# A 2:4 pruned matmul on one Trainium2 core: single half-tile loads, alternating VectorE steps, a halved weight piece, narrower last output pieces

## The chip, the core and the metric

The kernel runs on one core of one Trainium2 chip. A core has five engines with queues of their own: TensorE (PE; its weight loads are shown apart as PEld), VectorE (DVE), ScalarE (ACT), GpSimd (POOL) and SyncE (SP). SP and ACT also issue DMAs, which share 16 DMA engines. The metric is device microseconds of one launch, the median of several runs. Before the change it is 235.76 us (three runs, 235.59 to 236.01).

## The reference

x is 16 x 512 x 1024, w is 1024 x 1024, b has 1024 elements, all bf16. In every group of four consecutive rows of w, and in each column, the two elements of largest magnitude are kept and the others set to zero. Then x is multiplied with that pruned w, and b is added.

```
wg = w.reshape(G, M, D)                      # G = 256 groups of M = 4 rows
mag = jnp.abs(wg)
order = jnp.argsort(mag, 1)
thr = jnp.take_along_axis(mag, order[:, M - N:M - N + 1, :], 1)     # N = 2
mask = (mag >= thr).astype(w.dtype)
wp = (wg * mask).reshape(D, D)
return jnp.einsum("bsd,df->bsf", x, wp) + b
```

## The kernel before

The 8192 rows of x are 64 token tiles of 128. An output tile is 128 x 1024, made as two halves of 512 columns, one PSUM bank each. The contraction over 1024 is eight matmuls of 128.

**Pruning.** w is loaded so that the four members of a group lie on one partition (`wv`, L50): partition p, half g of the contraction (0 or 1), member m, column f. Five loads A to E bring it (L53). The work on it is cut into pieces `(g, first column, end column)` (L51). For each piece the magnitudes are made (token A, `abs_piece`, L109, on VectorE for pieces 0 and 2, on ScalarE for the others). Then `prep_piece` (token P, L120) issues seven VectorE steps: hi and lo (L127, L128: the larger and the smaller of each pair), two steps t (L131, L132: the smaller of the two hi, the larger of the two lo), thr (L134: the larger of these, which is the second largest magnitude of the four), mask (L136) and wp (L137: w times mask). Steps follow one another piece by piece. In the text, h, l, t, u, r, k, p stand for hi, lo, the two t, thr, mask and wp, with the number of the piece behind.

**The front.** While w is being pruned, the first T = 7 token tiles are computed directly from the pieces. x is loaded in half tiles (128 tokens x 512 columns, 128 KB; `load_x`, L73): x0 to x6 are the halves g = 0 of tiles 0 to 6; the halves g = 1 come later. TensorE transposes a half tile with four 128-wide transposes (token Tgt, `transpose_half`, L148), and ScalarE copies the result out of PSUM (L154). Then four matmuls per piece and tile (token Mit, `mm_piece`, L157) add piece i to the bank of tile t. All halves g = 1 go through bank 7, so each transpose of these waits for the copy before it. When the left output half of a tile is done, ScalarE moves it out (token V, L176), which frees the bank for the right half. Token S adds the bias to it on VectorE, token U copies pruned weights by four DMAs into the layout for the main phase (`unpack`, L142), token B issues a DMA transpose of x (`issue_batch`, L192). Eight matmuls on zeros (token W, L105) stand ahead of all.

The order of all this on every engine is the order of the tokens in the string `FRONT` (L208), since each instruction is kept in program order. An engine runs its own instructions strictly in that order.

**Loads.** L80 to L94 issue them on two queues: w_A in halves on SP and ACT, x0-1 on SP, x2-3 on ACT, w_B on SP, x4-5 on ACT, and then on SP x6, the g = 1 half of tiles 0-1, w_C, the g = 1 halves of tiles 2-3 and 4-6, w_D, w_E and the bias.

**The main phase.** Tiles 7 to 63 use x transposed by DMA and the unpacked weights: L248 for the tiles 7 to 11 and for the last tile, L286 for the others. VectorE adds the bias (L184), ACT's queue stores (L188). The last tile (`last_tile`, L256) is made in four pieces of 256 columns, each with its own eight matmuls, its add on VectorE (L264) and its store on SP's queue (L265).

The two lists that the change rewrites in the front stand so before:

```
pieces = [(0, 0, 128), (0, 128, 256), (0, 256, 512), (1, 0, 256), (1, 256, 512),
          (0, 512, 768), (0, 768, 1024), (1, 512, 1024)]
load_x(0, 0, 2)
load_x(0, 2, 4, nc.scalar)
load_w("B")
load_x(0, 4, 6, nc.scalar)
load_x(0, 6, 7)
```

Of the kernel before, what the change touches and what calls it, by code (L numbers as in the profile page):

```python
# [10 lines left out]
def kernel(  # L11
# [21 lines left out]
    FH = 512  # L33
# [3 lines left out]
    of = out.flatten_outer_dims()  # L37
# [3 lines left out]
    const = ctx.enter_context(tc.tile_pool(name="const", bufs=1))  # L41
    tmp = ctx.enter_context(tc.tile_pool(name="tmp", bufs=2))
# [4 lines left out]
    bank = [psum.tile([P, FH], fp32, name=f"bank{i}") for i in range(8)]  # L47


    wv = w.rearrange("(g p m) f -> p g m f", g=2, m=4)  # L50
    pieces = [(0, 0, 128), (0, 128, 256), (0, 256, 512), (1, 0, 256), (1, 256, 512),  # L51
              (0, 512, 768), (0, 768, 1024), (1, 512, 1024)]
    loads = {"A": (0, 0, 256), "B": (0, 256, 512), "C": (1, 0, 512), "D": (0, 512, 1024), "E": (1, 512, 1024)}  # L53
    w_ld = {k: const.tile([P, 4, c1 - c0], bf16, name=f"w_{k}") for k, (g, c0, c1) in loads.items()}
    wp_gh = {(g, h): const.tile([P, 4, FH], bf16, name=f"wp_{g}_{h}") for g in range(2) for h in range(2)}

    def w_of(i):
        g, c0, c1 = pieces[i]
# [14 lines left out]
    def load_x(g, ta, tb, eng=nc.sync):  # L73
        xt = const.tile([P, tb - ta, KH], bf16, name=f"xh_{g}_{ta}")
        src = xf[ta * P:tb * P, g * KH:(g + 1) * KH].rearrange("(t p) c -> p t c", p=P)
        K(eng.dma_start(xt[:], src))  # L76
        for t in range(ta, tb):
            xh[(g, t)] = xt[:, t - ta, :]

    load_w("A", nc.sync, 0, 2)  # L80
    load_w("A", nc.scalar, 2, 4)
    load_x(0, 0, 2)
    load_x(0, 2, 4, nc.scalar)
    load_w("B")
    load_x(0, 4, 6, nc.scalar)
    load_x(0, 6, 7)
    load_x(1, 0, 2)
    load_w("C")
    load_x(1, 2, 4)
# [3 lines left out]
    bias_sb = const.tile([P, Dout], bf16, name="bias_sb")  # L93
# [10 lines left out]
        for _ in range(n):  # L104
            K(nc.tensor.matmul(bank[7][:], lhsT=zeros[:, :P], rhs=zeros[:], start=True, stop=True))  # L105

    mags = {}

    def abs_piece(i, on_act):  # L109
        g, c0, c1 = pieces[i]  # L110
        n = c1 - c0
        mag = const.tile([P, 4, n], bf16, name=f"mag_{i}")[:]
        if on_act:
            K(nc.scalar.activation(mag, w_of(i), Act.Abs))  # L114
        else:
            K(nc.vector.tensor_single_scalar(  # L116
                mag.bitcast(u16), w_of(i).bitcast(u16), 0x7FFF, op=Alu.bitwise_and))
        mags[i] = mag

    def prep_piece(i):  # L120
        g, c0, c1 = pieces[i]
        n = c1 - c0
        mag = mags.pop(i)
        magv = mag.rearrange("p (a j) f -> p a j f", j=2)
        hi = tmp.tile([P, 2, FH], bf16, name="hi")[:, :, :n]
        lo = tmp.tile([P, 2, FH], bf16, name="lo")[:, :, :n]
        K(nc.vector.tensor_tensor(hi, magv[:, :, 0, :], magv[:, :, 1, :], op=Alu.max))  # L127
        K(nc.vector.tensor_tensor(lo, magv[:, :, 0, :], magv[:, :, 1, :], op=Alu.min))  # L128
        t1 = tmp.tile([P, FH], bf16, name="t1")[:, :n]
        t2 = tmp.tile([P, FH], bf16, name="t2")[:, :n]  # L130
        K(nc.vector.tensor_tensor(t1, hi[:, 0, :], hi[:, 1, :], op=Alu.min))  # L131
        K(nc.vector.tensor_tensor(t2, lo[:, 0, :], lo[:, 1, :], op=Alu.max))  # L132
        thr = tmp.tile([P, FH], bf16, name="thr")[:, :n]
        K(nc.vector.tensor_tensor(thr, t1, t2, op=Alu.max))  # L134
        mask = tmp.tile([P, 4, FH], bf16, name="mask")[:, :, :n]
        K(nc.vector.tensor_tensor(mask, mag, thr[:, None, :].to_broadcast([P, 4, n]), op=Alu.is_ge))  # L136
        K(nc.vector.tensor_tensor(wp_of(i), w_of(i), mask, op=Alu.mult))  # L137
# [19 lines left out]
    def mm_piece(i, t, start=False, stop=False):  # L157
        g, c0, c1 = pieces[i]
        o = c0 % FH
        for m in range(4):  # L160
            K(nc.tensor.matmul(  # L161
                bank[t][:, o:o + c1 - c0], lhsT=xT[(g, t)][:, m, :], rhs=wp_of(i)[:, m, :],
                start=start and m == 0, stop=stop and m == 3))
# [28 lines left out]
    def issue_batch(t0, nb):  # L192
# [13 lines left out]


    FRONT = """  # L208
        W W W W W W W W A0 A1 T00 T01 T02 T03 P0 M00 M01 M02 P1 T04 T05 A2 M03 M10 T06 M11 M04 M12 T10 M05 M06
        M13 M14 A3 T11 M15 M16 P2 M20 M21 A4 T12 M22 M23 M24 A5 T13 P3 M25 M26 M30 A6 T14 M31 M32 M33 A7  # L210
        P4 T15 M34 M40 M41 M42 V0 M43 V1 T16 M35 V2 M44 P5 B0 U00 U10 M45 V3 M50 V4 M36 V5 M51 M46 P6
        U01 M52 V6 M53 M54 M55 M56 M60 M61 M62 M63 M64 P7 U11 B1 B2 M65 M66 S0 S1 S2 S3 S4 S5 S6
    """
    ABS_ON_ACT = (1, 3, 4, 5, 6, 7)
    for tok in FRONT.split():
        k, n = tok[0], [int(c) for c in tok[1:]]
        if k == "W":
            warm(1)
        elif k == "A":
            abs_piece(n[0], n[0] in ABS_ON_ACT)  # L220
        elif k == "P":
            prep_piece(n[0])
        elif k == "T":
            g, t = n
            transpose_half(g, t, t if g == 0 else T)
        elif k == "M":
            i, t = n
            mm_piece(i, t, start=i in (0, 5), stop=i in (4, 7))
        elif k == "V":
            evac_act(n[0])  # L230
        elif k == "S":
            add_staged(n[0], 0)
        elif k == "U":
            unpack(*n)
        elif k == "B":
            issue_batch(*batches[n[0]])

    for t in range(T):
        mm_piece(7, t, stop=True)
        evac_dve(t, 1, t)  # L240
        store(t)

# [3 lines left out]
    def mm_nat(t, h, bk, c0=0, c1=FH):  # L246
        for kt in range(KT):
            K(nc.tensor.matmul(bank[bk][:, :c1 - c0], lhsT=xN[t][:, kt, :], rhs=wp_nat[h][:, kt, c0:c1],  # L248
                               start=kt == 0, stop=kt == KT - 1))

    def next_bank():
        bk = nbk[0] % 8
        nbk[0] += 1
        return bk

    def last_tile(t):  # L256
        o_sb = get_o(t)
        QW = FH // 2
        for h in range(2):
            for c0 in (0, QW):  # L260
                bk = next_bank()
                mm_nat(t, h, bk, c0, c0 + QW)
                f = slice(h * FH + c0, h * FH + c0 + QW)
                K(nc.vector.tensor_tensor(o_sb[:, f], bank[bk][:, :QW], bias_sb[:, f], op=Alu.add))  # L264
                K(nc.sync.dma_start(of[t * P:(t + 1) * P, f], o_sb[:, f]))  # L265
# [55 lines left out]
```

## Time and profile before

| what | us |
|---|---|
| median of three runs | 235.76 (235.59 to 236.01) |
| the profiled execution's own time | 236.1 |
| its span, first to last instruction | 234.3 |
| TensorE busy | 228.1 |
| VectorE busy | 105.7 |
| ScalarE busy | 18.5 |
| w_A landed (SP's half, ACT's half) | 3.64, 3.83 |
| x0-1, x2-3 landed | 5.33, 5.77 |
| x4-5, w_B, x6 landed | 7.57, 8.08, 8.45 |
| w_C, w_D, w_E landed | 10.72, 14.10, 16.48 |
| last store landed | 233.37 |

The span is the time between the first and the last recorded instruction of one profiled execution; what lies around it belongs to the measured time only. A matmul's recorded duration is longer than what it holds TensorE for, since matmuls overlap: in the main phase 512-wide matmuls are recorded with 379 ns each and start 216 ns apart. Starts, not durations, tell the rate. The same holds for VectorE's steps, so the timeline is read by starts.

### The profile page before, as it was taken

The numbers are of one execution on the slowest core, as the hardware profiler recorded it, in microseconds if no ns is written. First come the engines' busy times: TensorE is split into PE (matmuls) and PEld (weight loads), VectorE is DVE, ScalarE is ACT, GpSimd is POOL, SyncE is SP. The second block draws the span as 40 slices with busy tenths as digits, with TensorE's granted clock in tenths as the row PEclk, the third lists the DMA queues.
The fourth block names the chain that finished last, engine by engine and source line by source line (L and its number), as shares of the span: only waits on it lengthen the run. The fifth ranks groups of instructions, "written<-read, shape, count | busy, mean of one in ns | idle before, by whom it ended". The sixth has DMA issues, their size and how long they took to land.

```text
span 234.3 us, 2922 instructions
## 1 busy us (share of the span) xinstructions
PE 228.1 (97%) x1197; PEld 114.6 (49%) x1216; DVE 105.7 (45%) x189; ACT 18.5 (8%) x29; POOL 0.7 (0%) x6
## 2 busy tenths in 40 slices
PE   6999999999999999999999999999999999999994
PEld 2889844444444444444444444444444444444453
DVE  3999995342442343344244234334324424433433
ACT  3899000000000000000000000000000000000000
POOL 1000000000000000000000000000000000000000
DMA  6999799999822399216952289221996221122122
GB/s 174 352 243 236 170 210 187 279 209 349 239 93 92 93 213 276 90 48 160 286 151 77 90 215 278 90 92 55 260 304 195 85 90 73 61 90 92 45 90 90
DMA packets 75292, 38.19 MB, mean 163 GB/s; under 512 B 60176, under 2 KB 67088, under 8 KB 75280
## 3 DMA queue, kind: packets, MB, share of 16 engines
q1 hardware_dynamic: 65392, 20.84, 42.6%
q10 hardware_dynamic: 9888, 17.17, 20.3%
q8 instruction: 9, 0.15, 0.3%
q14 instruction: 3, 0.02, 0.0%
HBM read 4.19 MB, written 16.78 MB: 90 GB/s over the span
## 4 chain that ended last, share of the span: by engine, by line
PE 93%; DMA 3%; DVE 2%; issue 1%; SPq 0%
PE bank L286 75%; PE bank L161 9%; PE bank L248 9%; DMA w_B<-in_w_dram 3%; PE bank L152 1%; DVE mask L136 0%; DVE wp L137 0%; SPq L76 0%; SPq L69 0%; DVE mag L116 0%; DVE o_sb L264 0%; DVE hi L127 0%; DVE lo L128 0%; DVE thr L134 0%; DVE t L132 0%
## 5 line engine op out<-in xcount | busy, mean ns | idle before, releaser
L286 PE MATMUL bank<-wp_nat,xTb 128*128 128x512 bf16 x753 | 165.1, 379 | 0.8
L184 DVE TENSOR_TENSOR o_sb<-bank,bias_sb 128x512 bf16<-128x512 f32 x119 | 76.7, 686 | 119.9 <-PE bank L286 108.6
L286 PEld LDWEIGHTS <-xTb 128*128 128x128 bf16 x768 | 75.1, 98 | 90.6
L161 PE MATMUL bank<-wp,xT 128*128 128x256 bf16 (+2 forms) x223 | 26.6, 272 | 0.4
L161 PEld LDWEIGHTS <-xT 128*128 128x128 bf16 x224 | 19.5, 98 | 5.6 <-ACT xT L154 0.7
L248 PE MATMUL bank<-wp_nat,xTs 128*128 128x512 bf16 (+1 forms) x110 | 21.0, 348 | 0.1
L248 PEld LDWEIGHTS <-xTs 128*128 128x128 bf16 x112 | 11.0, 98 | 10.0
L286 PE MATMUL bank<-wp_nat,xTs 128*128 128x512 bf16 x47 | 10.5, 379 | 0.1
L154 ACT COPY xT<-bank 128x512 bf16<-128x512 bf16 x14 | 7.7, 589 | 1.8 <-PE bank L152 1.8
L286 PEld LDWEIGHTS <-xTs 128*128 128x128 bf16 x48 | 4.7, 97 | 5.7
L136 DVE TENSOR_TENSOR mask<-mag,thr 128x1024 bf16<-128x1024 bf16 (+2 forms) x8 | 5.5, 692 | 0.3
L152 PE MATMUL bank<-ident,xh 128*128 128x128 bf16 x56 | 4.8, 219 | 0.7 <-DMA xh<-in_x_dram 0.6
L152 PEld LDWEIGHTS <-xh 128*128 128x128 bf16 x56 | 3.9, 114 | 1.8 <-DMA xh<-in_x_dram 1.5
L105 PE MATMUL bank<-zeros 128*128 128x512 bf16 x8 | 3.5, 625 | 1.2 <-DVE zeros L97 1.2
L180 DVE TENSOR_TENSOR o_sb<-stage,bias_sb 128x512 bf16<-128x512 f32 x7 | 4.3, 682 | 0.0
L176 ACT COPY stage<-bank 128x512 f32<-128x512 f32 x7 | 3.8, 627 | 0.3 <-PE bank L161 0.3
L127 DVE TENSOR_TENSOR hi<-mag 128x512 bf16<-128x512 bf16 (+2 forms) x8 | 3.4, 420 | 0.4 <-ACT mag L114 0.3
L128 DVE TENSOR_TENSOR lo<-mag 128x512 bf16<-128x512 bf16 (+2 forms) x8 | 3.3, 417 | 0.0
L134 DVE TENSOR_TENSOR thr<-t,t 128x256 bf16<-128x256 bf16 (+2 forms) x8 | 2.3, 292 | 0.3
L105 PEld LDWEIGHTS <-zeros 128*128 128x128 bf16 x8 | 1.0, 140 | 2.8 <-issue 1.7
L131 DVE TENSOR_TENSOR t<-hi 128x256 bf16<-128x256 bf16 (+2 forms) x8 | 2.3, 284 | 0.0
L132 DVE TENSOR_TENSOR t<-lo 128x256 bf16<-128x256 bf16 (+2 forms) x8 | 2.3, 284 | 0.0
(21 smaller groups left out, 17.4 us busy)
## 6 DMA issues: line engine op xcount, KB each, us to landing
out_dram<-o_sb ACTq DMA_DIRECT2D x63, 256.0 KB, 3.4
wp_nat<-wp SPq DMA_DIRECT2D x16, 128.0 KB, 2.7
xh<-in_x_dram SPq DMA_DIRECT2D x3, 256.0 KB, 6.1
xh<-in_x_dram ACTq DMA_DIRECT2D x2, 256.0 KB, 5.2
w_C<-in_w_dram SPq DMA_DIRECT2D x1, 512.0 KB, 6.9
w_D<-in_w_dram SPq DMA_DIRECT2D x1, 512.0 KB, 7.9
w_E<-in_w_dram SPq DMA_DIRECT2D x1, 512.0 KB, 8.9
xh<-in_x_dram SPq DMA_DIRECT2D x1, 384.0 KB, 6.8
```

The source lines that it names most:

```text
L105: K(nc.tensor.matmul(bank[7][:], lhsT=zeros[:, :P], rhs=zeros[:], start=True, stop=True))
L127: K(nc.vector.tensor_tensor(hi, magv[:, :, 0, :], magv[:, :, 1, :], op=Alu.max))
L128: K(nc.vector.tensor_tensor(lo, magv[:, :, 0, :], magv[:, :, 1, :], op=Alu.min))
L136: K(nc.vector.tensor_tensor(mask, mag, thr[:, None, :].to_broadcast([P, 4, n]), op=Alu.is_ge))
L152: K(nc.tensor.transpose(dst[:, m, :], xv[:, m, :], ident[:]))
L154: K(nc.scalar.copy(xt[:], dst))
L161: K(nc.tensor.matmul(bank[t][:, o:o + c1 - c0], lhsT=xT[(g, t)][:, m, :], rhs=wp_of(i)[:, m, :], start=start and m == 0, stop=stop and m = ...
L176: K(nc.scalar.copy(st[:], bank[t][:]))
L180: K(nc.vector.tensor_tensor(get_o(t)[:, h * FH:(h + 1) * FH], stage.pop(t)[:], bias_sb[:, h * FH:(h + 1) * FH], op=Alu.add))
L184: K(nc.vector.tensor_tensor(get_o(t)[:, h * FH:(h + 1) * FH], bank[bk][:], bias_sb[:, h * FH:(h + 1) * FH], op=Alu.add))
L248: K(nc.tensor.matmul(bank[bk][:, :c1 - c0], lhsT=xN[t][:, kt, :], rhs=wp_nat[h][:, kt, c0:c1], start=kt == 0, stop=kt == KT - 1))
L286: K(nc.tensor.matmul(bank[bks[h]][:], lhsT=xN[t][:, kt, :], rhs=wp_nat[h][:, kt, :], start=kt == 0, stop=kt == KT - 1))
```

## The change

Five things are changed.

1. x0 to x4 are each loaded by a DMA of their own, in turn by SP's and ACT's queue; x5 and x6 come together on SP's queue, behind w_B. There are two DMAs more, and ACT's queue carries x1, x3 and x4 instead of x2-3 and x4-5.
2. The third piece, columns 256 to 512 of g = 0, is halved. There are nine pieces, and the numbers of those behind it move up by one: w_C gives pieces 4 and 5, w_D 6 and 7, w_E 8. The magnitudes of pieces 0, 2, 3 and 4 are made on VectorE (token a), the others on ScalarE (token A).
3. A piece's steps are tokens of their own, and the steps of a piece and of its forerunner alternate on VectorE: for example `r4 h5 k4 l5 p4`.
4. The order of the front is written anew with seven W instead of eight; transposes T00 to T04 stand ahead of the first matmul on a piece, and the loop behind the front, which computed the last piece, 7, now computes piece 8.
5. The last tile is made in pieces of 512, 256, 128 and 128 columns.

```
-    pieces = [(0, 0, 128), (0, 128, 256), (0, 256, 512), (1, 0, 256), (1, 256, 512),
+    pieces = [(0, 0, 128), (0, 128, 256), (0, 256, 384), (0, 384, 512), (1, 0, 256), (1, 256, 512),
               (0, 512, 768), (0, 768, 1024), (1, 512, 1024)]
+    H1 = 6
...
-    load_x(0, 0, 2)
-    load_x(0, 2, 4, nc.scalar)
+    load_x(0, 0, 1)
+    load_x(0, 1, 2, nc.scalar)
+    load_x(0, 2, 3)
+    load_x(0, 3, 4, nc.scalar)
     load_w("B")
-    load_x(0, 4, 6, nc.scalar)
-    load_x(0, 6, 7)
+    load_x(0, 4, 5, nc.scalar)
+    load_x(0, 5, 7)
     load_x(1, 0, 2)
     load_w("C")
...
+    def step(k, i):
...
+        if k == "h":
+            K(tt(new(i, "hi", [P, 2, FH])[:, :, :n], mv[:, :, 0, :], mv[:, :, 1, :], op=Alu.max))
+        elif k == "l":
+            K(tt(new(i, "lo", [P, 2, FH])[:, :, :n], mv[:, :, 0, :], mv[:, :, 1, :], op=Alu.min))
...
+        elif k == "k":
+            thr = wk[(i, "thr")][:, :n]
+            K(tt(new(i, "mask", [P, 4, FH])[:, :, :n], mag, thr[:, None, :].to_broadcast([P, 4, n]), op=Alu.is_ge))
+        elif k == "p":
+            K(tt(wp_of(i), w_of(i), wk[(i, "mask")][:, :, :n], op=Alu.mult))
...
     FRONT = """
-        W W W W W W W W A0 A1 T00 T01 T02 T03 P0 M00 M01 M02 P1 T04 T05 A2 M03 M10 T06 M11 M04 M12 T10 M05 M06
-        M13 M14 A3 T11 M15 M16 P2 M20 M21 A4 T12 M22 M23 M24 A5 T13 P3 M25 M26 M30 A6 T14 M31 M32 M33 A7
-        P4 T15 M34 M40 M41 M42 V0 M43 V1 T16 M35 V2 M44 P5 B0 U00 U10 M45 V3 M50 V4 M36 V5 M51 M46 P6
-        U01 M52 V6 M53 M54 M55 M56 M60 M61 M62 M63 M64 P7 U11 B1 B2 M65 M66 S0 S1 S2 S3 S4 S5 S6
+        W W W W W W W a0 A1 h0 l0 T00 t0 u0 T01 r0 k0 T02 p0 T03 T04 h1 M00 l1 t1 M01 u1 M02 r1 k1 M03 a2 p1 T05 T06
+        h2 l2 M04 t2 u2 M10 a3 T10 r2 h3 M05 k2 M11 M06 l3 M12 p2 M13 t3 T11 u3 A5 a4 M14 M15 r3 h4 M16 M20 k3 M21
+        l4 M22 M23 p3 T12 t4 M24 u4 M25 M26 r4 M30 h5 M31 k4 T13 M32 M33 l5 M34 p4 M35 A6 M36 T14 t5 M40 u5 r5 M41
+        h6 A7 M42 k5 T15 l6 M43 A8 p5 M44 t6 M50 u6 r6 M51 h7 M52 k6 M53 V0 l7 T16 V1 B0 U00 U10 p6 M45 M54 t7 u7 V2
+        M55 r7 h8 M46 V3 M60 k7 V4 M56 V5 l8 M61 V6 p7 U01 M62 M63 t8 u8 M64 r8 M65 M66 k8 M70 M71 p8 U11 B1 B2
+        M72 M73 M74 M75 M76 S0 S1 S2 S3 S4 S5 S6
     """
...
     for t in range(T):
-        mm_piece(7, t, stop=True)
+        mm_piece(8, t, stop=True)
...
     def last_tile(t):
         o_sb = get_o(t)
-        QW = FH // 2
-        for h in range(2):
-            for c0 in (0, QW):
+        for h, c0, c1 in ((0, 0, FH), (1, 0, 256), (1, 256, 384), (1, 384, FH)):
...
```

More of the change, by code (lines that the diff above doesn't have):

```diff
@@ L105, in warm, with new @@
             K(nc.tensor.matmul(bank[7][:], lhsT=zeros[:, :P], rhs=zeros[:], start=True, stop=True))
-    mags = {}
-    def abs_piece(i, on_act):
+    wk = {}
+    def new(i, name, shape):
+        wk[(i, name)] = tmp.tile(shape, bf16, name=name)
+        return wk[(i, name)]
+    def step(k, i):
         g, c0, c1 = pieces[i]
         n = c1 - c0
[L112 to L137, printed above, removed]
+        if k in "aA":
+            mag = const.tile([P, 4, n], bf16, name=f"mag_{i}")
+            wk[(i, "mag")] = mag
+            if k == "A":
+                K(nc.scalar.activation(mag[:], w_of(i), Act.Abs))
+            else:
+                K(nc.vector.tensor_single_scalar(
+                    mag[:].bitcast(u16), w_of(i).bitcast(u16), 0x7FFF, op=Alu.bitwise_and))
+            return
@@ new lines, in step @@
+        mag = wk[(i, "mag")][:]
+        mv = mag.rearrange("p (a j) f -> p a j f", j=2)
+        tt = nc.vector.tensor_tensor
+        if k == "h":
+            K(tt(new(i, "hi", [P, 2, FH])[:, :, :n], mv[:, :, 0, :], mv[:, :, 1, :], op=Alu.max))
+        elif k == "l":
+            K(tt(new(i, "lo", [P, 2, FH])[:, :, :n], mv[:, :, 0, :], mv[:, :, 1, :], op=Alu.min))
+        elif k == "t":
+            hi = wk[(i, "hi")]
+            K(tt(new(i, "t1", [P, FH])[:, :n], hi[:, 0, :n], hi[:, 1, :n], op=Alu.min))
+        elif k == "u":
+            lo = wk[(i, "lo")]
+            K(tt(new(i, "t2", [P, FH])[:, :n], lo[:, 0, :n], lo[:, 1, :n], op=Alu.max))
+        elif k == "r":
+            K(tt(new(i, "thr", [P, FH])[:, :n], wk[(i, "t1")][:, :n], wk[(i, "t2")][:, :n], op=Alu.max))
+        elif k == "k":
[3 more added lines that the diff above has]
+            K(tt(wp_of(i), w_of(i), wk[(i, "mask")][:, :, :n], op=Alu.mult))
@@ L208 @@
     FRONT = """
-        W W W W W W W W A0 A1 T00 T01 T02 T03 P0 M00 M01 M02 P1 T04 T05 A2 M03 M10 T06 M11 M04 M12 T10 M05 M06
-        M13 M14 A3 T11 M15 M16 P2 M20 M21 A4 T12 M22 M23 M24 A5 T13 P3 M25 M26 M30 A6 T14 M31 M32 M33 A7
-        P4 T15 M34 M40 M41 M42 V0 M43 V1 T16 M35 V2 M44 P5 B0 U00 U10 M45 V3 M50 V4 M36 V5 M51 M46 P6
-        U01 M52 V6 M53 M54 M55 M56 M60 M61 M62 M63 M64 P7 U11 B1 B2 M65 M66 S0 S1 S2 S3 S4 S5 S6
+        W W W W W W W a0 A1 h0 l0 T00 t0 u0 T01 r0 k0 T02 p0 T03 T04 h1 M00 l1 t1 M01 u1 M02 r1 k1 M03 a2 p1 T05 T06
[4 more added lines that the diff above has]
+        M72 M73 M74 M75 M76 S0 S1 S2 S3 S4 S5 S6
     """
-    ABS_ON_ACT = (1, 3, 4, 5, 6, 7)
     for tok in FRONT.split():
@@ L218 @@
             warm(1)
[L219 to L222, printed above, removed]
+        elif k in "Aahlturkp":
+            step(k, n[0])
         elif k == "T":
@@ L227 @@
             i, t = n
-            mm_piece(i, t, start=i in (0, 5), stop=i in (4, 7))
+            mm_piece(i, t, start=i in (0, H1), stop=i == H1 - 1)
         elif k == "V":
@@ L257, in last_tile @@
         o_sb = get_o(t)
-        QW = FH // 2
-        for h in range(2):
-            for c0 in (0, QW):
[L261 to L265, printed above, removed]
+        for h, c0, c1 in ((0, 0, FH), (1, 0, 256), (1, 256, 384), (1, 384, FH)):
+            bk = next_bank()
+            mm_nat(t, h, bk, c0, c1)
+            f = slice(h * FH + c0, h * FH + c1)
+            K(nc.vector.tensor_tensor(o_sb[:, f], bank[bk][:, :c1 - c0], bias_sb[:, f], op=Alu.add))
+            K(nc.sync.dma_start(of[t * P:(t + 1) * P, f], o_sb[:, f]))
     for bi, (t0, nb) in enumerate(batches):
```

## The prediction

> **What bounds the kernel now.** I read the page's busy times first, then the chain that ended last, in order of time, then the timeline of the first 35 and the last 8 us.
>
> ```profile
> PE 228.1 (97%) x1197; PEld 114.6 (49%) x1216; DVE 105.7 (45%) x189; ACT 18.5 (8%) x29; POOL 0.7 (0%) x6
> ```
>
> TensorE is busy for 97% of the span, and none of its 1024 column blocks is removed. Only its waits can change: before the first transpose, in the front, and after the last matmul. The chain shows where they are:
>
> ```profile
> 1.75 6.33 DMA w_B<-in_w_dram
> ...
> 10.82 0.70 DVE wp L137
> 11.52 0.04 issue
> 11.56 1.03 PE bank L161 x8
> ...
> 34.44 4.96 PE bank L248 x23
> ```
>
> Up to 11.56 us the chain is w_B's landing (1.75 + 6.33 = 8.08) and VectorE's eight steps on piece 2; from there TensorE alone. The timeline gives the steps:
>
> ```profile
> 5.24 0.43 DVE L136 TENSOR_TENSOR mask<-mag,thr 128x512 bf16<-128x512 bf16 x1
> ...
> 5.70 0.43 DVE L137 TENSOR_TENSOR wp<-w_A,mask 128x512 bf16<-128x512 bf16 x1
> ...
> 6.05 0.28 DVE L127 TENSOR_TENSOR hi<-mag 128x256 bf16<-128x256 bf16 x1
> ...
> 10.74 1.06 ACT L114 ACTIVATE mag<-w_C 128x1024 bf16<-128x1024 bf16 x1 [0.27 <-DMA w_C<-in_w_dram]
> ...
> 11.83 0.42 DVE L127 TENSOR_TENSOR hi<-mag 128x512 bf16<-128x512 bf16 x1 [0.32 <-ACT mag L114]
> ```
>
> wp needs the mask and starts 0.03 after it ends (5.24 + 0.43, then 5.70). The next piece's hi needs neither and starts 0.08 before wp ends (5.70 + 0.43 = 6.13, hi at 6.05). So a step with an independent follower holds VectorE for its duration less 83 ns, one with a dependent follower for its duration plus 34: 117 ns apart. With these two rules, the rows' durations and the landings I laid out the front step by step (VectorE's 60 steps, ScalarE's copies, 280 matmuls and transposes): every weight piece comes out within 0.02 us of the trace, every transpose within 0.06, and TensorE's first matmul of L248 at 34.30 (trace: 34.28, record by record; some records are missing, so the chain says 34.44). In that layout VectorE is a second bound: the last piece ends at 28.20 and its first 512-wide matmul starts at 28.24, 0.08 late.
>
> **The change, part by part.**
>
> *Loads.* Two more DMAs, issued at 0.45 to 0.5 us each on queues with room. The eight DMA semaphores go round, so the ninth DMA waits for the first: x5-7 now waits for w_A (landed 3.64 and 3.83), w_C for x1, E for x4. These issues hide behind the transfers in front (the tightest is x5-7: issued by 4.4, and w_B's bytes before it last beyond 6); without that cover each costs its 0.5 us. What counts is the bytes in front. Of the DMA issues (KB, us to landing):
>
> ```profile
> w_B<-in_w_dram SPq DMA_DIRECT2D x1, 256.0 KB, 6.3
> ...
> xh<-in_x_dram SPq DMA_DIRECT2D x1, 128.0 KB, 6.0
> ```
>
> w_B, issued at 1.75, landed at 8.08; x6, issued at 2.47 behind it, at 8.45. x0 should land near 4.2 instead of 5.33 (an estimate: half of its old transfer), x4 near 6.6 (between the old second ACT load at 5.77 and the old third at 7.57). In front of w_B stand 128 KB less, at 350 GB/s (window 6 to 7 us) 0.37 us: 7.72 instead of 8.08. But x5 moves behind w_B: x5-7 ends the same 1408 KB that x6 ended, so it lands at 8.45 as x6 did, and w_C at 10.72. T05 needs x5, so TensorE stands at 8.50 with nine of its 0.224 us units done, where before it had eleven done at 8.57. The earlier x0 buys nothing: 0.73 us of idle time follow x4's work. Bounds for each landing: 0.3 us either way, since two 256 KB loads issued together landed 0.44 apart (5.33, 5.77).
>
> *One warm-up less* saves nothing; TensorE waits for x0 anyway.
>
> *Alternation and the halved piece.* Dependent followers fall from 26 to 13: -1.5 us of VectorE. Halving piece 2 costs 3.44 instead of 2.85 (eight steps at 128 and at 256 columns): +0.59. Piece 4's abs moves from ScalarE to VectorE: +0.34, but VectorE's waits for loads and for ScalarE's abs fall from 0.61 to 0.34. VectorE ends its pieces near 27.34 instead of 28.20, and the 0.08 stall there goes. But the order puts piece 3's steps between piece 4's, and abs 4 waits for w_C. From there to p5 the holds are 0.34 (a4), 1.50 (r3 h4 k3 l4 p3), 0.73 (t4 u4 r4), 1.90 (h5 k4 l5 p4), 0.73, 1.29 (h6 k5 l6) and p5's 0.69: 7.18. With a4 at 10.74, p5 ends at 17.92, M50 starts at 17.97, and what is behind it on TensorE is 23 groups of 256 columns at 0.436, a transpose at 0.224 and 28 matmuls of 512 at 0.2158: 16.30. The front ends at 34.27: **-0.01**. Two more chains are nearly as late. x5-7 at 8.45 brings TensorE to M50 at 17.83, 0.14 spare. w_B at 7.72 frees VectorE for a4 at 10.70, 0.04 spare. The 28 added narrow matmuls cost 28 x (2 x 55.9 - 109) ns = 0.08, inside that sum.
>
> Against the alternation speaks the Trainium skill, VectorE: DVE Perf Modes, "The DRAIN you can't avoid": after every op the pipe must empty before the next, and chaining differently does not help. The hi row above starts 0.08 before its forerunner ends, with nothing left to wait for, so the trace disagrees for independent neighbours (the page itself says further down that an op that isn't held starts earlier). It is a rival below.
>
> *The last tile.*
>
> ```profile
> 229.30 2.85 SPq L265 DMA_DIRECT2D out_dram<-o_sb  x4
> ...
> 231.36 0.42 DVE L264 TENSOR_TENSOR o_sb<-bank,bias_sb 128x256 bf16<-128x256 f32 x1 [0.45 <-PE bank L248]
> ```
>
> The matmul time is the same (8 x 216 + 8 x 109 + 16 x 56 = 3.49; before 32 x 109). The last add shrinks from 0.42 to 0.29 (512 wide 0.69, 256 wide 0.42: 1.05 ns a column). But SP needs 0.34 for an issue and 0.11 to the next (0.046, a semaphore wait of 0.017, 0.046). The 256-wide store is issued 0.43 before the last matmul ends, the third no earlier than 0.02 after, the last no earlier than 0.46 after; now it is 0.48 after. So 0.01 of the 0.13 arrives. The last transfer halves (64 KB took 1.56 to land): -0.05, taken between -0.2 (add and transfer both tell) and +0.1 (256 B rows not shown here).
>
> **Sum:** -0.01 - 0.05 = -0.06. Against the profiled execution (span 234.3, its time 236.1, 1.8 around the span) that is 236.0; the median of the runs is 235.76, 0.3 below that execution, and gets 235.7. As the front's end is the latest of three chains 0.04 to 0.14 apart, one that is late tells and one that is early does not; for landings spread by 0.3 I add 0.1: **235.8**.
>
> **Rivals.**
>
> *Loads land earlier* (faster). For: from 4 to 6 us the queues moved only 265 and 232 GB/s, with 350 to 370 after; single half tiles may fill that. With every load 0.5 sooner or more, VectorE never waits after p0: p5 ends at 17.58, the front 0.35 earlier, and that is a floor: VectorE sets it. With the best tail, -0.55: 235.2. Against: the same bytes on the same queues.
>
> *w_B gates piece 1* (slower). In VectorE's order abs 2 stands before p1, so everything from piece 1's last step on waits for w_B; M10 and all of TensorE's later groups wait behind it. It decides once w_B lands after 7.76, and then costs its lateness one for one: unchanged at 8.08 +0.32, at 8.4 +0.64, 236.3. For: its issue is 0.5 later, behind x2. Against: 128 KB less in front.
>
> *The clock stays low* (slower). The warm-ups start 427 ns apart for 512 columns, the later ones 216, and the first transposes, at 5.38, 56 for 128: the fast rate came after eight warm-ups, 3.4 us. Seven end at 4.17, and then TensorE works in pieces. If the slow rate lasts to 8.5 it is hidden by the wait for x5; to 10 it costs 0.8: 236.5. The granted clock in the windows is 1.00 throughout and shows none of this.
> The Trainium skill, TensorE: Matmul & The Clock Gate, Part 1, puts the release at some 3.4 us of sustained activity; by it seven would be short, and the transposes would have to make it up.
>
> *Alternation overlaps nothing* (the change doesn't do what it says). Then every alternated step pays the 117 ns, VectorE ends at 31.5 and the front 3.3 later: 239.0. The skill's drain rule would give this; the hi row speaks against it.
>
> *x5-7 lands late* (slower): decides after 8.59; at 9.2, +0.6: 236.3.
>
> **Numbers.** 0.2% is 0.47 us, about what a measurement of this kernel tells from no change. Forecast 0.46; earlier loads 0.22 (faster); w_B 0.16, clock 0.10, no overlap 0.04, x5-7 0.02 (slower, 0.32). The range 235.1 to 236.7 holds the forecast (alone 235.4 to 236.2), the faster case and most of w_B and the clock.
>
> **What would show it.** T05 waiting for x5-7 until 8.4 to 8.6, TensorE with no wait at M20, M50 starting within 0.1 of p5's end near 17.97, VectorE's last piece near 27.3, the last store issued 0.46 after the last matmul. Wrong if w_C or w_B land more than 0.3 off, if alternated neighbours start later than 0.08 before their forerunner ends, or if transposes start over 100 ns apart.

## The result, and the profile after

The changed kernel took 237.01 us (median of 20 runs, 235.94 to 243.35), the kernel before 235.89 beside it (20 runs): a ratio of 1.0046, 95% interval 1.0031 to 1.0061. The forecast was 235.8, in a range of 235.1 to 236.7. Every ratio here leaves out executions over 1.5% above the fastest of their kernel (of the changed kernel's twenty that is one, 243.35). The profiled execution of the changed kernel took 238.36 (span 236.57), the second longest of the twenty, against 236.10 (span 234.32): 2.26 us more, in three places, but only 1.1 us more in the medians.

| place | before | after | difference |
|---|---|---|---|
| front end (first matmul of tiles 7 to 11) | 34.28 | 34.93 | +0.65 |
| wait for the first eight-tile transpose xTb | none | 51.98 to 53.72, less one matmul of 0.216 | +1.52 |
| last matmul's end | 231.32 | 233.51 | +2.19 (the two above make 2.17) |
| last matmul's end to the span's end | 2.99 | 3.06 | +0.07 |

From the page's busy times of the changed kernel:

```profile
PE 229.3 (97%) x1224; PEld 116.1 (49%) x1243; DVE 105.6 (45%) x198; ACT 17.7 (7%) x28; POOL 0.7 (0%) x6
```

VectorE is as busy as before, with nine more instructions; TensorE has 1.2 us more. The chain that ended last, in order of time (start, length, what), tells more:

```profile
1.74 4.13 DMA xh<-in_x_dram
5.92 1.47 PE bank L163 x12
7.39 1.71 PE bank L172 x16
9.09 0.77 PE bank L163 x8
...
15.03 0.59 ACT xT L165
15.62 0.96 ACT mag L124
...
16.61 0.42 DVE hi L133
...
25.31 2.53 DMA wp_nat<-wp
...
27.88 1.90 DVE o_sb L191 x3
...
31.88 21.80 DMA xTb<-in_x_dram
...
53.72 9.46 PE bank L294 x43
...
230.02 3.51 PE bank L258 x32
...
233.55 0.29 DVE o_sb L272
```

Before, the chain began with w_B and was TensorE's from 11.56 on. Now it begins with x2, runs through transposes, ScalarE's copies and its abs of w_D into VectorE, then through the copies of the weights and one row of 21.80 us, the first eight-tile transpose xTb; TensorE comes last. That row is the news: before, xTb was issued at 31.59 and landed at 50.83, 0.72 us ahead of its use at 51.55; now it was issued at 31.88 and landed at 53.68. The tile view of xTb gives the time from issue to landing for the six transposes into it (smallest, median, largest), first of the kernel before, then after, with who waited:

```profile
DMA to landing us min/median/max: 11.8/13.3/19.2
```

```profile
  PE bank L294: 1.4, 1
...
DMA to landing us min/median/max: 12.5/13.4/21.8
```

The largest is the first one in each. The later ones, 2 MB too, take some 13 us; the first was slow before the change and became slower.

The timeline from 30 to 36 us shows what runs beside it, first before, then after:

```profile
31.59 15.71 SPq L197 DMA_TRANSPOSE xTb<-in_x_dram  x1
...
33.03 3.53 ACTq L188 DMA_DIRECT2D out_dram<-o_sb  x5
```

```profile
31.88 19.27 SPq L208 DMA_TRANSPOSE xTb<-in_x_dram  x1
...
32.80 3.36 ACTq L199 DMA_DIRECT2D out_dram<-o_sb  x6
```

The first output store follows the transpose's issue by 0.93 us (before by 1.45: 31.59, 33.03), because VectorE and with it the first finished tile are ahead while the transpose's issue, behind the copies of the weights, is 0.29 late.

### The profile page after: what moved, and what is told of

The parts are those of the page before. It is cut to its first block, busy times and chain, and to the rows that moved or that the text cites. A ratio compares the mean times of both kernels' runs of the same rounds, so it can differ in the third digit from the quotient of the medians.

```text
span 236.6 us, 2985 instructions
## 1 busy us (share of the span) xinstructions
PE 229.3 (97%) x1224; PEld 116.1 (49%) x1243; DVE 105.6 (45%) x198; ACT 17.7 (7%) x28; POOL 0.7 (0%) x6
## 4 chain that ended last, share of the span: by engine, by line
PE 79%; DMA 12%; DVE 4%; SPq 2%; issue 1%; ACT 1%
PE bank L294 74%; DMA xTb<-in_x_dram 9%; PE bank L172 3%; DMA xh<-in_x_dram 2%; PE bank L258 1%; PE bank L163 1%; SPq L155 1%; DMA wp_nat<-wp 1%; DVE o_sb L191 1%; DVE mask L146 1%; DVE wp L148 1%; DVE lo L135 1%; DVE hi L133 0%; ACT mag L124 0%; ACT xT L165 0%
## 5 line engine op out<-in xcount | busy, mean ns | idle before, releaser
L172 PE MATMUL bank<-wp,xT 128*128 128x128 bf16 (+2 forms) x251 | 26.8, 266 | 0.1
L172 PEld LDWEIGHTS <-xT 128*128 128x128 bf16 x252 | 20.9, 101 | 4.3
L258 PE MATMUL bank<-wp_nat,xTs 128*128 128x512 bf16 (+2 forms) x110 | 21.0, 348 | 0.1
L258 PEld LDWEIGHTS <-xTs 128*128 128x128 bf16 x112 | 10.4, 98 | 10.7
L163 PE MATMUL bank<-ident,xh 128*128 128x128 bf16 x56 | 6.2, 262 | 0.7 <-DMA xh<-in_x_dram 0.7
L146 DVE TENSOR_TENSOR mask<-mag,thr 128x512 bf16<-128x512 bf16 (+2 forms) x9 | 5.6, 627 | 0.1
L133 DVE TENSOR_TENSOR hi<-mag 128x256 bf16<-128x256 bf16 (+2 forms) x9 | 3.5, 391 | 0.5 <-ACT mag L124 0.4
L135 DVE TENSOR_TENSOR lo<-mag 128x256 bf16<-128x256 bf16 (+2 forms) x9 | 3.5, 388 | 0.0
L143 DVE TENSOR_TENSOR thr<-t,t 128x128 bf16<-128x128 bf16 (+2 forms) x9 | 2.5, 275 | 0.2
L141 DVE TENSOR_TENSOR t<-lo 128x128 bf16<-128x128 bf16 (+2 forms) x9 | 2.4, 269 | 0.0
L138 DVE TENSOR_TENSOR t<-hi 128x128 bf16<-128x128 bf16 (+2 forms) x9 | 2.4, 269 | 0.0
L272 DVE TENSOR_TENSOR o_sb<-bank,bias_sb 128x128 bf16<-128x128 f32 (+2 forms) x4 | 1.7, 425 | 1.0 <-PE bank L258 1.0
(22 smaller groups left out, 16.2 us busy)
```

Source lines behind the costliest of these rows:

```text
L133: K(tt(new(i, "hi", [P, 2, FH])[:, :, :n], mv[:, :, 0, :], mv[:, :, 1, :], op=Alu.max))
L135: K(tt(new(i, "lo", [P, 2, FH])[:, :, :n], mv[:, :, 0, :], mv[:, :, 1, :], op=Alu.min))
L146: K(tt(new(i, "mask", [P, 4, FH])[:, :, :n], mag, thr[:, None, :].to_broadcast([P, 4, n]), op=Alu.is_ge))
L163: K(nc.tensor.transpose(dst[:, m, :], xv[:, m, :], ident[:]))
L172: K(nc.tensor.matmul(bank[t][:, o:o + c1 - c0], lhsT=xT[(g, t)][:, m, :], rhs=wp_of(i)[:, m, :], start=start and m == 0, stop=stop and m = ...
```

## Experiments

Eighteen kernels ran, each beside the kernel before, 6 to 12 times. Two questions came out of the profile: does the half clock rate at the start, or something else, make the front late, and is xTb late because stores run beside it?

**Warm-ups.** An eighth `W` put back into the changed kernel, and one taken out of the kernel before:

```
e1_w8:         -  W W W W W W W a0 A1 ...      +  W W W W W W W W a0 A1 ...
e2_before_w7:  -  W W W W W W W W A0 A1 ...    +  W W W W W W W A0 A1 ...
```

> The changed kernel with eight warm-ups again instead of seven. Clock theory (the seventh warm-up ends too early, the transposes and the first matmuls run at half rate until 9.5 us, and the front ends 0.65 us later for it): transposes start 56 ns apart from the first or second on, the front ends at 34.2 to 34.4, and the time falls by about 0.65, to 236.3. Transpose theory (the landing of the first 8-tile x transpose, 53.7 us in the profile of the changed kernel, sets the start of the main phase, whatever the front does): the front may end sooner, but TensorE then waits the longer for that landing, and the time stays at 236.8 to 237.0.

> The kernel before with seven warm-ups instead of eight, nothing else. Clock theory: the transposes at 5.4 us start over 100 ns apart, the front ends 0.4 to 0.7 later than 34.28, and the time rises to 236.3 to 236.6. Transpose theory: the front had 0.7 us in hand before the first 8-tile transpose is needed, the landing stays near 50.8, and a later front costs its lateness as well, but the spread of the runs stays as small as before (1.0 us over the runs); without a clock effect 235.9.

e1: 236.87 (235.98 to 238.06), ratio 1.0049, 1.0029 to 1.0068. Its front ended at 34.02, 0.26 earlier than in the kernel before, and nothing of that arrived: xTb landed at 52.09, 20.85 us after its issue, and was needed at 51.29. e2: 235.80, ratio 1.0001, 0.9983 to 1.0019: a warm-up less costs the kernel before nothing. So the half rate matters to the front of the changed kernel at most, and the wait for xTb is independent of it.

**The unpacking copies moved.** To issue xTb earlier, the copies U01 and U11 went to ScalarE's queue:

```
-  K(nc.sync.dma_start(wp_nat[h][:, 4 * g + j, :], ...))
+  K((nc.scalar if h else nc.sync).dma_start(wp_nat[h][:, 4 * g + j, :], ...))
```

> The changed kernel with the eight copies of the right half of the unpacked weights issued on ACT's queue instead of SP's, so that SP can issue the first 8-tile transpose some 5 us sooner. Transpose theory: it lands before 50 us, TensorE has no wait at the start of the main phase, and the time falls by what the runs wait there, to about 236.4, with the spread of the runs smaller. Clock theory alone: 237.0, unchanged.

> Both edits, eight warm-ups and the copies on ACT's queue. If clock and transpose together are the loss: front end at 34.2 to 34.4, no wait for the transpose, 235.6 to 235.9, which is what the prediction's own steps gave. If it stays above 236.3, something else in the change costs time.

246.18 (ratio 1.0452, 1.0415 to 1.0488) and 245.93 (1.0427, 1.0387 to 1.0467): a wait of their own. In e3's profile the last two copies on ScalarE's queue waited for a DMA semaphore that xTb's landing (43.98) set free and landed at 49.85 and 51.52; TensorE started no matmul from 43.94 to 49.89 and only one from there to 51.56. Neither theory is touched by the time. xTb, with its first store 18 us behind it, still took 16.90 and 19.93: the copies ran beside it instead.

**Stores placed later in the program.** The first seven stores, each two or four tiles later in the program:

```
     evac_dve(t, 1, t)
-    store(t)
+    if t >= 2:
+        store(t - 2)
```

> The changed kernel with eight warm-ups, and the store of each of the first seven tiles issued two tiles later (behind the add of the tile after next, about 1.2 us later). Collision theory (VectorE ends its pieces sooner, so the first stores start sooner and run beside the 8-tile transpose of x, which then lands later): first store 1.8 us or more behind the transpose's issue, landing 17.5 to 19.5 us after issue instead of 20.9, no wait at the start of the main phase, time 235.5 to 236.0. Rival (the transpose itself runs slower in the changed kernel, for example by where its data or its issue stand, whatever the stores do): landing still 20.5 to 22 us after issue, time 236.8.

> The same with the stores four tiles later (about 2.4 us). Collision theory: landing 16.5 to 18.5 us after issue, no wait, 235.5 to 235.9; the landing falls from 0 to 2 to 4 tiles. Rival: as without the delay, 236.8.

> The changed kernel as it is, with seven warm-ups, and the stores two tiles later. Collision theory: the wait at the start of the main phase goes, the time falls to 235.8 to 236.4; what is left above the eight-warm-up version is the price of the clock (0 to 0.6). Rival: 237.0.

This edit does nothing: ScalarE's queue holds no other work there, so each store still waits for its own tile alone, and instruction for instruction on every engine e5 and e6 are e1, and e7 is the changed kernel. They are repeats: 236.73, 236.66 (e1: 236.87) and 236.68 (ratio 1.0033, 1.0010 to 1.0056; the first time 1.0046). What they add is two sights of one program. In e7's profile (236.70, its median) the store came 1.50 us after xTb's issue, xTb landed after 18.08, and TensorE did not wait; the front ended at 34.81. In the first profile these were 0.93, 21.80, 1.52 and 34.93.

**xTb issued late in the kernel before.** Two unused copies of 128 KB each on SyncE's queue ahead of it:

```
+    scr = const.tile([P, 2, FH], bf16, name="scr")
-  ... P7 U11 B1 B2 M65 ...
+  ... P7 U11 X0 X1 B1 B2 M65 ...
+    elif k == "X":
+        K(nc.sync.dma_start(scr[:, n[0], :], wp_gh[(1, 1)][:32, :, :]))
```

> The kernel before, with two more copies of pruned weights into an unused tile on SP's queue ahead of the first 8-tile transpose, so that this is issued about 1.3 us later and the stores run beside it sooner. Collision theory: it lands 20 to 22 us after issue, at 52.5 to 54, TensorE waits 1 to 2 us there, the time rises to 236.8 to 237.6. Rival: landing 17.5 to 19.3 us after issue as in the kernel before, at 50.5 to 51.9, and the time rises by at most 0.3.

242.22 in the median of six (239.53 to 249.63); ratio 1.0194, 1.0163 to 1.0226, from the lowest three. The profiled execution, 245.98, is not one of these; in it the store came 0.34 us behind xTb's issue, xTb took 26.31, and TensorE waited from 51.31 to 58.81. Behind that wait its matmuls started 427 ns apart instead of 216 until 63.85. The direction is collision's, the size above what it expected. By lead of the transpose over the first store, the profiles up to here (two later ones fit in: e11 with 1.62 and 18.43, e18 with 2.28 and 17.32):

| run | lead, us | issue to landing, us |
|---|---|---|
| e2_before_w7 | 1.80 | 17.37 |
| e7_lag2 | 1.50 | 18.08 |
| before | 1.45 | 19.24 |
| after | 0.93 | 21.80 |
| e5, e6, e1 | 0.79, 0.69, 0.66 | 21.17, 21.00, 20.85 |
| e8_before_b1late | 0.34 | 26.31 |

**Stores really held back.** One ScalarE copy that needs the seventh tile, ahead of all seven stores, with room for the tiles that then wait:

```
-    outp = ... bufs=10
+    outp = ... bufs=13
     for t in range(T):
         mm_piece(8, t, stop=True)
         evac_dve(t, 1, t)
-        store(t)
+    hold = const.tile([P, 16], bf16, name="hold")
+    K(nc.scalar.copy(hold[:], out_tiles[T - 1][:, Dout - 16:]))
+    for t in range(T):
+        store(t)
```

> The changed kernel, with one 16-element ScalarE copy of the seventh tile's output placed ahead of the first seven stores on ScalarE's queue, and 13 output buffers instead of 10: ScalarE reaches a store only when VectorE has finished tile 6 (36.4 in the changed kernel's profile instead of 32.8), so the first eight-tile transpose has some 4.5 us to itself instead of 0.93. Two earlier edits that moved the stores in the program did not do this, since ScalarE's queue held nothing ahead of them. If the stores beside it are what lengthened the transpose (the four runs with a head start of 1.45 to 1.80 landed 17.4 to 19.2 us after issue, the four with 0.34 to 0.93 us 20.9 to 26.3), it lands 16 to 18.5 us after issue, before TensorE needs it (52.2), the wait of 1.5 us is gone, and the time is about 235.6 to 236.3. If it is late for another reason (the issue itself, the loads, the order of VectorE's work), it still lands 21 to 22 us after issue, the wait stays, and the time is about 237.0.

> The same with an eighth warm-up matmul, with which the front end ended at 33.6 to 34.0 instead of 34.9 in three profiles. Collision: no wait for the first eight-tile transpose, and the earlier front end reaches the end for the first time: 235.76 less 0.3 to 0.6, plus 0.07 for the tail, so about 235.2 to 235.6, faster than both kernels. Rival (late for another reason): the wait of 0.8 to 1.0 us stays, 236.7.

In e9 the stores begin 5.74 us behind xTb's issue. The timeline of ScalarE from 30 to 46 us, and the tile view of xTb:

```profile
36.59 0.20 ACT L252 COPY hold<-o_sb 128x16 bf16<-128x16 bf16 x1 [12.08 <-DVE o_sb L195]
36.60 7.69 ACTq L199 DMA_DIRECT2D out_dram<-o_sb  x7
```

```profile
DMA to landing us min/median/max: 12.0/12.5/16.2
```

The first transpose landed 13.07 us after its issue (e10: 13.40; the 16.2 is a later one), no one waits for it, and TensorE goes from one batch to the next without a gap. What the queues moved from 30 to 56 us, in 40 slices of 0.65 us, after and then e9:

```profile
GB/s 189 222 192 200 156 145 198 239 159 146 166 177 191 134 103 132 184 187 182 292 345 365 360 365 291 110 26 58 69 72 71 225 290 290 201 152 234 218 289 290
```

```profile
GB/s 199 206 186 152 224 279 290 290 290 290 290 291 290 290 290 353 403 435 363 386 355 120 143 164 227 228 290 290 295 119 345 285 235 183 290 290 290 96 0 120
```

Alone, the transpose runs at 290 GB/s, slice after slice from 33.9 us on; in the changed kernel both together move 103 to 239 from 33.9 to 42.3. The packets by queue show how they share. In e9 the transpose moves 283 KB in each us from 34 to 39, in packets of 256 bytes and 18 ns, and the stores, issued from 36.60 on, move their first packet only at 39.92, when the transpose has 2028 of its 2048 KB behind it. In the changed kernel the transpose moves 208 KB from 34 to 35; then the first store's packets come, and it moves 82 to 133 KB per us until 40 beside 26 to 76 KB of stores, and 42 to 44 KB from 42 to 45 beside 206 to 312. The head start shows in bytes: ahead of the first store's packet the transpose had moved 1118 KB in e2, 760 in the kernel before, 323 in the changed one and 80 to 171 in e1, e5 and e6. Why the two together are slower than the transpose alone stays open: from 47 to 50 us of the changed kernel, with 14 to 20 KB of stores per us left, the transpose moved 17 to 53 KB per us, in packets of 87 to 98 ns. Delayed stores cost nothing either: they land at 41.3 to 46.7 instead of 42.0 to 50.5 for the first six. So it is shown that the stores beside it make xTb late. The time is not explained by that: e9 236.60 (235.79 to 237.53), ratio 1.0033, 1.0018 to 1.0049; e10 236.16 (235.45 to 238.18), ratio 1.0022, 1.0003 to 1.0041. The rest had to be looked for in the front and the tail.

**The tail.** The changed last tile alone in the kernel before, and the old last tile in e10:

```
e11:  -  for h in range(2): for c0 in (0, QW): ...
      +  for h, c0, c1 in ((0, 0, FH), (1, 0, 256), (1, 256, 384), (1, 384, FH)): ...
e12:  the same, turned round
```

> The kernel before with the changed last tile alone (512, 256, 128 and 128 columns instead of four times 256). If the tail is worth what the changed kernel's profile shows (3.06 us from the last matmul's end to the span's end against 2.99), the time is 235.8 to 235.9, no difference. My forecast's term was -0.05. If the narrower last pieces cost more than the one profile shows (one more transfer's fixed time), it is 236.2 or more, and part of the loss belongs to the tail.

> The kernel with eight warm-ups and the held stores, with the last tile as it was before. Beside the run with the narrow tail it differs by the tail alone: by the two profiles -0.07, so 235.1 to 235.5 if the collision theory holds, 236.6 if it does not.

e11: 235.71, ratio 0.9992, 0.9980 to 1.0004. e12: 236.59, ratio 1.0031, 1.0014 to 1.0049, with no wait for xTb (13.37). In the time the narrow tail is neither gain nor loss. In the profiles it gains what was forecast: from the last matmul's end to the span's end 2.94 in e11 against 2.99 before, 3.06 in e10 against 3.12 in e12. The 0.07 lost at the end of the changed kernel is something else: the last store's landing and the span's end lie 0.94 or 0.95 apart in the six profiles with 105 DMAs (before, e2, e11, e14, e15, e18) and 1.07 or 1.08 in the fourteen with two DMAs more, whatever their last tile. There SyncE waits in five steps, two semaphores each, the eight of the DMAs among them; with 105 DMAs the last store has a semaphore of the third step, with 107 one of the first, and two more steps, 0.13 us, stand behind its landing.

**What sets the front.** In e9's profile, without the wait, the chain in order of time is this:

```profile
0.73 2.88 DMA w_A<-in_w_dram
3.61 0.02 issue
3.63 0.39 SPq L77
...
4.58 7.06 DMA w_C<-in_w_dram
...
16.22 1.47 PE bank L172 x12
...
20.95 14.34 PE bank L172 x104
35.29 17.27 PE bank L261 x80
52.56 176.12 PE bank L297 x816
```

SyncE's issue of x5-7 (x5 and x6 in one load, at 3.63) waits for w_A's landing, w_C's issue stands two issues behind it, w_C lands at 11.63, and from there the chain is VectorE's and TensorE's to the end. Over the profiles of the changed order a simple rule holds, its two distances read from these same profiles: the front ends 23.50 us after w_C lands, or 24.80 after the first transpose of the second half (T10) starts, whichever is later. Us:

| run | w_C landed | T10 starts | rule | front end |
|---|---|---|---|---|
| after | 10.79 | 10.14 | 34.94 (T10) | 34.93 |
| e1_w8 | 10.53 | 9.15 | 34.03 (w_C) | 34.02 |
| e3_uact | 10.73 | 9.31 | 34.23 (w_C) | 34.23 |
| e4_w8_uact | 11.29 | 9.20 | 34.79 (w_C) | 34.78 |
| e5_w8_lag2 | 10.24 | 9.00 | 33.80 (T10) | 33.80 |
| e6_w8_lag4 | 10.13 | 8.76 | 33.63 (w_C) | 33.62 |
| e7_lag2 | 11.31 | 9.89 | 34.81 (w_C) | 34.81 |
| e9_hold | 11.63 | 9.05 | 35.13 (w_C) | 35.13 |
| e10_w8_hold | 11.90 | 9.27 | 35.40 (w_C) | 36.28 |
| e12_w8_hold_oldtail | 10.69 | 9.36 | 34.19 (w_C) | 34.19 |

In e10 alone w_D, landing at 16.85 (14.1 to 14.2 in the changed kernel, e3, e12 and e13), came as a third: its chain runs from w_D's landing through ScalarE's abs. The old order has the same two bounds. Three profiles of it end the front 23.56 behind w_C (10.70 to 10.74); where w_C was early (e11 at 9.92, e8 at 10.00), and later in e18, the front ends 24.45 to 24.48 behind T10. So the new order is worth 0.06 us behind w_C and costs 0.34 behind T10, and a late load is handed on one for one. Behind the front little varies: in the thirteen profiles without a wait for xTb (before, e2, e7, e9 to e18) the span ends 199.98 to 200.16 us after the front. Four kernels were to test the rule:

```
e13:  -  load_x(1, 0, 2)   load_w("C")   load_x(1, 2, 4)
      +  load_w("C")   load_x(1, 0, 2)   load_x(1, 2, 4)
e14:  the five half tiles loaded as before: load_x(0, 0, 2), load_x(0, 2, 4, nc.scalar), load_w("B"),
      load_x(0, 4, 6, nc.scalar), load_x(0, 6, 7)
e15:  the kernel before, with the hold and 13 buffers of e9
e16:  +  load_x(1, 0, 2)   load_x(1, 2, 4)   load_w("C")
```

(e13, e14 and e16 are e10 with that edit; e16's three loads now stand in this order.)

> Eight warm-ups and held stores, with w_C issued one place earlier, ahead of the second half of tiles 0 and 1 (256 KB). If w_C's landing sets the front end, it lands some 0.7 us earlier (256 KB at about 350 GB/s), at 9.4 to 11.2, the front end ends 23.5 behind it, 33.0 to 34.7, and the time falls by 0.3 to 0.7 from the 236.16 of the kernel with w_C in its old place: 235.5 to 235.9. If TensorE's order bounds it, it then waits for the second half of tiles 0 and 1, which lands 0.7 later, the distance grows to 24 or more, and the time stays at 236.2 or rises.

> Eight warm-ups and held stores, with the five half tiles loaded as in the kernel before (two and two, then one), so that w_C's issue does not stand behind one more load and the wait for a slot that x5-7 has. What is left of the change is VectorE's order, the halved piece and the narrow tail. If the loads are what costs, w_C lands at 9.9 to 10.7 as in the profiles of before, the front end lies at 33.4 to 34.3, and the time is 235.2 to 235.7. If the order of VectorE's work costs, the front end lies at 34.5 or later and the time stays at 236.2 to 236.6.

> The kernel before with the ScalarE copy ahead of its first seven stores and 13 output buffers alone. Its first eight-tile transpose already landed 0.72 us ahead of its use, so by the collision theory the transpose lands 13 us after issue instead of 19.2, some 6 us ahead of its use, and the time stays: 235.5 to 235.8. If holding the stores costs something by itself (later stores, ScalarE's copy), it is 236.1 or more, and that part of the 236.2 to 236.6 of the three kernels with held stores is not the front end's.

> Eight warm-ups and held stores, with w_C one place later, behind the second half of tiles 2 and 3 (256 KB). If w_C's landing sets the front end: it lands at 11.0 to 12.5, the front end lies 23.5 behind it, 34.5 to 36, and the time is 0.6 to 0.8 above the kernel with w_C in its place, 236.8 to 237. If it does not, 236.2.

- e13: 237.96, ratio 1.0098, 1.0070 to 1.0127. w_C landed earlier, at 10.11, but T10 now started at 10.88, and the front ended at 35.70 (rule 35.68, by T10). w_C alone is not the bound; the load that gives way takes its place.
- e16: 237.13, ratio 1.0056, 1.0036 to 1.0075. w_C at 11.91, front end 35.40 (rule 35.41, by w_C).
- e15: 235.69, ratio 0.9997, 0.9985 to 1.0008. Its xTb landed 11.82 us after issue instead of 19.24, and the time stayed: holding the stores is free, and worth nothing where xTb was in time.
- e14: 237.06, ratio 1.0054, 1.0027 to 1.0081, with a wide spread (235.56 to 239.63). In its profile, the slowest of its runs, the new order puts T04 ahead of the first piece's matmuls, and T04 stands from 6.1 to 8.2 for a load that is late in the old grouping; TensorE then runs at half rate until 14 us, and the front ends at 37.84, 0.98 over the rule. w_C, with the old loads and issued at 3.87, landed at 11.42 in it, later than the 9.9 to 10.7 expected. The order needs the new loads, so this run does not say what the loads alone cost.

The head of e13's chain, in order of time, with the half tiles that took w_C's place:

```profile
4.78 6.06 DMA xh<-in_x_dram
10.83 0.05 issue
10.88 0.41 PE bank L163 x4
```

Two runs were left: does the half rate explain the rest, and does the kernel before hang on w_C too?

```
e17:  -  ... T01 r0 k0 T02 ...   M03 a2 p1 T05 T06
      +  ... T01 r0 k0 W W T02 ...   M03 a2 p1 W W T05 T06      (in e10)
e18:  -  load_x(1, 0, 2)   load_w("C")
      +  load_w("C")   load_x(1, 0, 2)                          (in the kernel before)
```

> Eight warm-ups and held stores, with two more warm-up matmuls ahead of tile 2's transpose and two ahead of tile 5's. If a clock that stays at half rate is what is left of the loss, the first transpose of the second half starts by 9.4 in its profile, the front end is w_C's landing plus 23.5, and the median falls from 236.16 to 235.6 or 235.8. If w_C's landing is what is left, the median stays at 236.1 to 236.5; if the filling matmuls themselves delay the transposes behind them (0.43 us each at half rate), it rises above that.

> The kernel before with w_C issued one place earlier, ahead of the second half of tiles 0 and 1. If the kernel before hangs on w_C (its landing plus 23.56 us in three profiles, 23.91 in the one where it landed at 9.92), w_C lands at about 10.0, the front end at 33.8 instead of 34.3, and the time falls by 0.4 to 235.3. If its order of work bounds it or the second half of tiles 0 and 1, now at 10.7, takes w_C's place, it is 235.7 or more.

e17: 236.76, ratio 1.0048, 1.0025 to 1.0071. Its profiled execution is its fastest, 235.78: no half rate after the warm-ups, w_C at 10.24, front end 33.74 (rule 33.74), no wait for xTb. Even this best case is no faster than the median of the kernel before (235.79). The filling bought nothing in the median; whether it removed a half rate there and cost as much itself, the times do not tell. e18: 237.00, ratio 1.0054, 1.0035 to 1.0073: the second half of tiles 0 and 1 landed at 11.52, T10 started at 11.56, and the front ended at 36.04. The kernel before is as closely balanced between two loads, as its expectation's second case had it.

## Why the prediction was wrong

*The step that failed* is the sum: "-0.01 - 0.05 = -0.06", and "for landings spread by 0.3 I add 0.1". It stopped at the front's end and carried that to the last matmul as if nothing in between could move; it took the spread of the landings from two loads of one execution (0.44 apart), where the executions differ by far more; and it put the two added DMAs at nothing, which cost 0.13 at the kernel's end.

- *Behind the front.* xTb had 0.72 us in hand, in the trace of before, and no step or rival of the prediction looked at it. In the profiled execution it cost 1.52 of 2.26 us, and it also took back the earlier front ends of e1, e5 and e6 (33.62 to 34.02): their main phase began at 51.86 to 52.13 whatever the front did. That stores running beside xTb cause the wait is shown by the hold (13 us instead of 21.8, no wait, in e9, e10 and e12). In the medians its share is small: with the hold 1.0033 and 1.0022 to 1.0031, without it 1.0033 to 1.0046 and 1.0034 to 1.0049 (seven and eight warm-ups); these intervals overlap.
- *w_C at 10.72.* The layout from it was right: forecast front end 34.27, which is w_C plus 23.55, and measured 23.50. The landing was the mis-sized term: 10.13 to 11.90 in the ten profiles of the table, where 0.3 either way was allowed. Four of the ten lie at 11.29 or later; in five profiles of the kernel before and its variants with the old order of loads (e2, e8, e11, e15) none lies above 10.74. In these five w_C lands 1.49 to 1.52 us behind the load ahead of it, in seven of the ten 1.38 to 1.48, but 2.42, 2.84 and 2.68 in e4, e9 and e10.
- *Clock stays low* (0.10, 236.5). It happened in the profiled execution: +0.65 through T10, within the 0.8 that the rival gave for a slow rate to 10 us (by w_C, at 10.79, the front would have ended at 34.29). That it weighs in the medians is not shown: eight warm-ups gave 1.0049 against 1.0046 for seven, and with the stores held 1.0022 and 1.0031 against 1.0033, within each other's intervals. The transposes show it in the timeline, first of the kernel before, then of the changed one:

```profile
5.38 1.08 PE L152 MATMUL bank<-ident,xh 128*128 128x128 bf16 x16 [0.64 <-DMA xh<-in_x_dram]
...
9.47 0.39 PE L152 MATMUL bank<-ident,xh 128*128 128x128 bf16 x4
```

```profile
4.15 1.05 PE L163 MATMUL bank<-ident,xh 128*128 128x128 bf16 x8
...
5.92 1.47 PE L163 MATMUL bank<-ident,xh 128*128 128x128 bf16 x12 [0.71 <-DMA xh<-in_x_dram]
...
8.89 0.97 PE L163 MATMUL bank<-ident,xh 128*128 128x128 bf16 x8
...
10.14 0.39 PE L163 MATMUL bank<-ident,xh 128*128 128x128 bf16 x4
```

  After the change they start 107 ns apart in the first three groups (56 before), and TensorE's starts are 56 apart only from 9.64 us on, though it worked without a gap from 5.92. The last row of each is T10. The Trainium skill, TensorE: Matmul & The Clock Gate, Part 1, says that the rate follows a free-running window of about 3.4 us of activity. The 3.7 us from 5.92 to 9.64 do not contradict that, and a free-running window would also make the rate differ from execution to execution, which it did: e7, the same program, had starts 56 apart from 4.8 us on. No run here shows the window itself.
- *w_B gates piece 1*: it landed at 7.06, and at 6.66 to 7.65 in the ten profiles of the table, always ahead of the 7.76 at which it decides. *Loads land earlier*: w_B and x5-7 did (7.76 against 8.45), w_C did not, and w_C counts.
- *Alternation overlaps nothing*: wrong, as argued. In the timeline of the changed kernel, where neighbouring pieces alternate:

```profile
9.08 0.42 DVE L146 TENSOR_TENSOR mask<-mag,thr 128x512 bf16<-128x512 bf16 x1
...
9.42 0.28 DVE L135 TENSOR_TENSOR lo<-mag 128x256 bf16<-128x256 bf16 x1
...
9.62 0.42 DVE L148 TENSOR_TENSOR wp<-w_B,mask 128x512 bf16<-128x512 bf16 x1
```

  lo starts 0.08 before the mask ends, wp 0.08 before lo ends, although wp needs that mask: the step in between hides the wait. VectorE gained what the two rules said: with w_C at 10.69 (e12) its last piece ends at 27.22, with 10.72 before at 28.19. The front did not, since TensorE's work behind w_C and T10 still sets its end.
- *One warm-up less saves nothing*: right (e2). *The tail*: forecast -0.05, and by itself it was worth that (e11 and e10, -0.05 and -0.06), with nothing to be seen in the time. The last store was issued 0.50 after the last matmul instead of 0.49, and its transfer took 1.49 us from issue to landing instead of 1.56. The changed kernel's end still came 0.07 later, by the 0.13 of the two added DMAs.

What remains: with the wait, the tail and the hold excluded, the kernels with held stores (e9, e10, e12, e17) are 0.22 to 0.48% slower than before, 0.5 to 1.1 us. About 0.1 of it is the two added DMAs. The rest must lie in the front, if what follows the front is as constant in all executions as in the thirteen profiles; there it comes by the landing of w_C or, in e10, of w_D. Why these land later more often with single half tiles stays open: w_C is issued at 4.49 to 4.87 instead of 3.59 to 3.85, but its landing varies by more than that, ten profiles against five do not separate the two, and e14's 11.42 came with the old loads. No version beats the kernel before.

## What to carry to other kernels

A gain ahead is worth what the next large transfer leaves of it: follow a change past the stage that it touches, to the first transfer that has little in hand, and ask what will now start beside it. When two or three chains end within some tenths of each other, price each load's landing with the spread between executions, one for one, since none of the gains adds up and every lateness does. Two more DMAs are not free either, even where their issues hide: look at what waits for their semaphores, up to the kernel's end. And moving a DMA later in the program text delays nothing unless its queue has something to wait for: give it an instruction that needs the later event.

## What the runs showed of the hardware

- A 2 MB DMA transpose from DRAM landed 11.8 to 13.4 us after its issue where the first store was issued 4.7 to 5.9 us behind it (eight profiles), 17.3 to 19.2 at 2.28 to 1.45 us (five), 20.9 to 21.8 at 0.93 to 0.66 us (four), and 26.3 at 0.34 (one profile, far above its median). Six stores of 256 KB ran beside it (seven at 0.34). Both together moved less than the transpose alone; held back in e9, the same stores cost it nothing and landed no later.
- A transpose under way keeps a later store waiting: the store's first packet moved 1.5 to 1.8 us after its issue where it was issued up to 0.8 us behind the transpose, 2.4 at 0.93, and 3.1 to 4.8 from 1.45 on.
- DMA semaphores couple the queues: in the changed kernel the seventh store on ScalarE's queue has the semaphore of xTb on SyncE's and is issued at 53.76, right behind xTb's landing at 53.68; in e9 at 43.95, behind 43.93. In e3, where copies that TensorE needs stood behind such a wait, the main phase began 9.1 us later than its front allowed.
- After standing still for 2.0 us (e14), 5.6 (e3) and 7.3 (e8) TensorE restarted at half rate, 107 ns for 128 columns or 427 for 512, and kept it for 4 to 6 us; after 1.5 us at 53.72 in the changed kernel it went on at 216.
- Single DMA packets of 1 KB on the load queue took up to 1.24 us in e9 (w_C at 11.63), 1.99 in e10 (11.90) and 1.15 in e12 (10.69), against 0.70 in the kernel before (10.72), where most take some 45 ns. Whether these make w_C late was not tried.
